# Chunk starts set by ScalarE and low weight parts by identity products, in a linear-attention and mixer kernel

## The chip, the cores and the metric

The kernel runs on one core of a Trainium2 chip. The core has a TensorE (PE, matmuls into PSUM; its weight loads are counted apart as PEld), a VectorE (DVE), a ScalarE (ACT), a GpSimd (POOL) and a SyncE (SP), whose queue issues all DMAs here. Each engine works through its own list of instructions in order and waits on semaphores for the others. The metric is device time in microseconds, the median of three runs.

## The reference

Three layers follow each other, all in fp32, with batch 4, 8 heads, 768 tokens and 48 channels a head:

```python
f = 1.0 / (1.0 + np.exp(-f_logit))
for t in range(S):                                     # gated linear attention
    state = f[:, :, t, :, None] * state + einsum('bhd,bhe->bhde', k[:, :, t], v[:, :, t])
    y[:, :, t] = einsum('bhd,bhde->bhe', q[:, :, t], state)
h = np.maximum(x @ w_in, 0.0)                          # x: [4, 768, 384], w_in: [384, 1024]
u, v = h[..., :512], h[..., 512:]
v_s = einsum('ts,bsd->btd', w_spatial, normalised(v)) + b_spatial[None, :, None]
x = (u * v_s) @ w_out
h = np.maximum(x.T @ w_tok1, 0.0) @ w_tok2             # per batch, over tokens
u = x + h.T
out = u + np.maximum(u @ w_ch1, 0.0) @ w_ch2           # 384 -> 1536 -> 384
```

## The kernel before

**Numbers.** Dense products are made from two parts of each fp32 operand: a high part `h` in the type fp32r (which TensorE takes in one pass) and a low part `l = a - h`. `mm3` (L149) issues three products for one: high by high, high by low, low by high. The weights arrive as fp64 (all but `w_sp`), so `rounded` (L57) makes an fp32 weight from two words with three DVE operations (L65, L68, L78), two on ACT (L72, L74) and one on POOL (L73). `split_weight` (L100) then casts the high part on ACT (L115, for `w_sp` L121) and subtracts on an engine that its caller names (L124): POOL for `w_in` (9 pieces, 6 of 384 columns and 3 of 256), `w_sp` (12 of 384) and `w_out` (4 of 384). `staged` (L129) runs such a piece in four steps, so that a few pieces are under way together; their staging tiles (`wsa`, `wst`) have three buffers each.

**Attention.** A unit is one batch, one half of the tokens (384) and one pair of heads, 4 x 2 x 4 = 32 units. Its input `fkq` holds logits, keys and queries, 128 x 3 x 384, brought by one DMA (the first unit's by three). ACT takes the sigmoid of the logits into `fs` (L369). `chunked` (L218) cuts the 384 tokens into three chunks of 128. DVE copies each chunk's first decay into `first` (L225, 128 x 3), sets those places of `fs` to zero (L226), and scans (L227): the running product `pc` of the decays restarts at each chunk. POOL copies the three end products to `pend` (L230). DVE clamps them at 1e-20 (L232), inverts them (L233) into `last`, scans backwards from them (L234) and multiplies keys and queries by both scans in one operation (L237, 128 x 768). PE transposes the keys (L243), multiplies keys by queries (L252), builds the state increments (L266, L267), and adds the outputs up in `py` (L297, L302, L308); POOL masks the 128 x 128 products (L257); DVE carries the state along (L277, L288, L290). The result is split into `xh` (ACT, L380) and `xl` (DVE, L381). `least`, the smallest of the end products, is looked at once, and a second, general program runs only if it is below 1e-20; it does not run here.

**First phase.** `s1` makes the hidden layer from `xh`, `xl` (products `pv`, `pu`), `s23` mixes tokens with `wsph`, `wspl` (`ps`), gates, and multiplies by `wouth`, `woutl` (`px`). Attention of the next batch, `s1` and `s23` of this batch and the conversion of weights are woven together by step counts (`weave`, L141). Batch 0's first attention half is woven with `w_in`, the second with `w_sp`, the first loop pass with `w_out`; the fp64 weights of the second phase are rounded during the passes that follow.

**Second phase.** Token and channel products of the last layer, from about 470 us on. It is a dense stream of matmuls with three-part products.

**What sets the order.** The program is built by a layer that assigns semaphores and, from a modelled timeline at build time, also chooses in which order each engine's instructions stand. A change of one instruction therefore moves others. The tag `m` of PSUM (pool `ps_m`, three buffers) serves `pv`, `pu`, `ps` and `px`.

Of the kernel before, what the change touches and what calls it, by code (L numbers as in the profile page):

```python
# [18 lines left out]
def tile_kernel(ctx, tc, fkqs, v, w_in, w_sp, b_sp, w_out, w_t1, w_t2, w_c1, w_c2, out):  # L19
# [28 lines left out]
    ident = const.tile([P, P], F32, name="ident")  # L48
    least = const.tile([P, 1], F32, name="least")
    flag = const.tile([1, 1], I32, name="flag")  # L50
# [48 lines left out]

    def split_weight(pool, stage, src, name, n, cols, eng, first=0, order=None):  # L100

        wide = src.dtype == mybir.dt.uint64
        h = pool.tile([P, n, cols], F32R, name=name + "h")
        l = pool.tile([P, n, cols], F32R, name=name + "l")
        if wide:
            src = src.bitcast(U32)
        srcr = src.rearrange("(n p) c -> n p c", p=P)

        def piece(i, c0, width):
            sl = (slice(None), i, slice(c0, c0 + width))  # L110
            at = stage.tile([P, WST], U32, tag="wsa", name=f"{name}sa{i}{c0}")
            a = at[:, :width]
            if wide:
                a = yield from rounded(stage, a, srcr[first + i], c0, width, f"{name}{i}{c0}")
                nc.scalar.copy(h[sl], a)  # L115
                yield
            else:
                a = f32(a)
                nc.sync.dma_start(out=a, in_=srcr[first + i][:, c0 : c0 + width])
                yield  # L120
                nc.scalar.copy(h[sl], a)  # L121
                yield
                yield
            eng.tensor_tensor(out=l[sl], in0=a, in1=f32(h[sl]), op=ALU.subtract)  # L124

        where = [(i, c0, min(WST, cols - c0)) for i in range(n) for c0 in range(0, cols, WST)]
        return h, l, [partial(piece, *x) for x in (order(where) if order else where)]

    def staged(pieces):  # L129

        gens = []

        def step(n):
            if n < len(pieces):
                gens.append(pieces[n]())
            for g in gens[max(0, n - 3) : n + 1]:
                next(g, None)

        return [partial(step, n) for n in range(len(pieces) + 3)]

# [16 lines left out]
    def body(general):  # L157
# [32 lines left out]
        if not general:  # L190
# [3 lines left out]
            )  # L194
            nc.gpsimd.memset(nhalf, -0.5)
        first, last = (attp.tile([P, W], F32, name=x) for x in ("first", "last"))
        states = [attp.tile([P, 128], F32, name=f"state{i}") for i in range(4)]
# [20 lines left out]
        def chunked(u, b, hf, p, fs, fkq, vt):  # L218
            ki, qi = fkq[:, 1, :], fkq[:, 2, :]
            n0 = hf * NCW  # L220
# [3 lines left out]
            gc, pc = pg[:, 0, :], pg[:, 1, :]  # L224
            nc.vector.tensor_copy(first[:, ::C], fs[:, :W:C])  # L225
            nc.vector.memset(fs[:, ::C], 0.0)  # L226
            nc.vector.tensor_tensor_scan(  # L227
                out=pc, data0=fs[:, :W], data1=first, initial=0.0, op0=ALU.mult, op1=ALU.add
            )
            nc.gpsimd.tensor_copy(pend[:, b * NP + p, n0 : n0 + NCW], pc[:, C - 1 :: C])  # L230
            ends = last[:, C - 1 :: C]
            nc.vector.tensor_scalar(out=ends, in0=pc[:, C - 1 :: C], scalar1=LOW, scalar2=None, op0=ALU.max)  # L232
            nc.vector.reciprocal(ends, ends)  # L233
            nc.vector.tensor_tensor_scan(  # L234
                out=gc[:, ::-1], data0=fs[:, W:0:-1], data1=last[:, ::-1], initial=0.0, op0=ALU.mult, op1=ALU.add
            )
            nc.vector.tensor_tensor(out=fkq[:, 1:, :], in0=fkq[:, 1:, :], in1=pg, op=ALU.mult)  # L237
            yield
# [75 lines left out]
        def scanned(u, b, hf, p, fs, fkq, vt):  # L314
# [15 lines left out]
            last = at3.tile([P, D], F32, tag=f"z{p}", name=f"z{u}")  # L330
            ki, qi, fs = fkq[:, 1, :], fkq[:, 2, :], fs[:, :W]
            for e in range(D):
# [19 lines left out]
        def att_unit(b, hf, p):  # L352

            u = f"{b}{hf}{p}"
            t0 = hf * W
            fkq = at3.tile([P, 3, W], F32, tag="fkq", name=f"fkq{u}")
            if (b, hf, p) == (0, 0, 0):
                for i in range(3):
                    nc.sync.dma_start(out=fkq[:, i, :], in_=fkqs[b, p, hf, :, i, :])
            else:  # L360
                nc.sync.dma_start(out=fkq, in_=fkqs[b, p, hf])
# [6 lines left out]
            fs = at2.tile([P, W + 1], F32, tag="fs", name=f"fs{u}")  # L368
            nc.scalar.activation(fs[:, :W], fkq[:, 0, :], AF.Sigmoid)  # L369
            core = scanned if general else chunked  # L370
# [75 lines left out]
        def s23(b):  # L446
# [39 lines left out]


        winh, winl, steps = split_weight(
            wr, wst, w_in, "win", NK, DFF, nc.gpsimd, order=lambda x: sorted(x, key=lambda y: -y[1])
        )  # L490
        weave(att(half(0, 0)), staged(steps))
        bb = const.tile([P, S], F32, tag="bb", name="bb")
        nc.sync.dma_start(out=bb, in_=b_sp.unsqueeze(0).to_broadcast([P, S]))
        wsph, wspl, st_a = split_weight(wl, wst, w_sp, "wsp", NCH, S, nc.gpsimd)
        wouth, woutl, st_b = split_weight(wl, wst, w_out, "wout", NJ, DM, nc.gpsimd)
        s10, a01, sa = s1(0, 0), att(half(0, 1)), staged(st_a)
# [250 lines left out]
```

## Time and profile before

| | |
|---|---|
| median of 3 runs | 825.38 us (825.36 to 826.94) |
| the profiled execution's own time | 828.73 us |
| its span in the trace | 827.0 us |
| PE busy | 765.1 us (93%) |
| DVE busy | 443.2 us (54%) |
| ACT busy | 274.6 us (33%) |
| POOL busy | 240.0 us (29%) |
| chain that ended last | PE 66%, DVE 17%, DMA 6%, issue 5% |

The shares of the whole span say little, since the stages differ: the 40 slices of the page and the busy times by stretch show which engine has no room in which stretch. Durations of matmuls in the trace overlap, since they are pipelined; the distance from one start to the next is what one costs. The chain names, going back from the last instruction, what released each step; "issue" is time in which the profile shows no releaser.

### The profile page before, as it was taken

What the parts mean: (1) busy time and instruction counts of PE and PEld (TensorE: products, weight loads), DVE (VectorE), ACT (ScalarE), POOL (GpSimd) and SP (SyncE); (2) the same over time, 40 slices, a digit from 0 to 9 for tenths busy, and PEclk for the clock granted to TensorE, in tenths of its full rate; (3) what the DMA queues carried; (4) which work ended last, traced back from release to release, by engine and by line L of the source; (5) the groups of instructions that cost most, each with busy time, mean ns of one, the idle gap of its engine ahead of it and who ended that gap; (6) DMA issues with size and microseconds to landing.
All of it is one profiled execution on the core that took longest, in us unless ns stands there. A gap on an engine that the chain in (4) does not pass through costs nothing.

```text
span 827.0 us, 12669 instructions
## 1 busy us (share of the span) xinstructions
PE 765.1 (93%) x4785; PEld 707.5 (86%) x4785; DVE 443.2 (54%) x916; ACT 274.6 (33%) x590; POOL 240.0 (29%) x290
## 2 busy tenths in 40 slices
PE   3468698999989999999999999999999999999996
PEld 2357577787778888899899999999999999999996
DVE  6997979989898874864464352122122212222211
ACT  4554535445452433323552341112112311111110
POOL 5786835535471112110580340004001210001000
PEclk9659689999989999999999999999999999999999
DMA  7473446575644331120341230002000200000000
GB/s 240 132 219 112 146 127 207 169 255 181 220 132 149 107 104 39 58 82 23 117 134 48 87 115 30 1 1 86 1 29 1 86 1 29 1 1 31 3 28 33
DMA packets 39846, 73.67 MB, mean 89 GB/s; under 512 B 5216, under 2 KB 29664, under 8 KB 39776
## 3 DMA queue, kind: packets, MB, share of 16 engines
q1 hardware_dynamic: 39776, 72.77, 27.7%
q8 instruction: 40, 0.66, 0.3%
q14 instruction: 30, 0.25, 0.1%
HBM read 54.66 MB, written 15.73 MB: 85 GB/s over the span
## 4 chain that ended last, share of the span: by engine, by line
PE 66%; DVE 17%; DMA 6%; issue 5%; POOL 2%; ACT 1%; SPq 1%; DVEq 0%; POOLq 0%; ACTq 0%
PE po L644 18%; PE p L155 8%; PE p L153 8%; PE p L154 8%; PE ps L153 2%; PE ps L155 2%; PE ps L154 2%; PE pa L252 2%; DVE pg L227 2%; PE px L153 2%; PE px L154 2%; PE py L302 2%; PE px L155 2%; PE py L308 1%; DVE state L277 1%
## 5 line engine op out<-in xcount | busy, mean ns | idle before, releaser
L632 DVE SCALAR_TENSOR_TENSOR hl<-p,hh 128x384 fp32r<-128x384 f32 x96 | 53.4, 557 | 189.6 <-ACT hh L631 189.6
L631 ACT ACTIVATE hh<-p 128x384 fp32r<-128x384 f32 x96 | 47.1, 492 | 198.1 <-PE p L155 198.1
L644 PE MATMUL po<-hl,wc2h 128*128 128x384 f32 x288 | 97.2, 338 | 0.0
L644 PE MATMUL po<-hh,wc2l 128*128 128x384 f32 x288 | 96.7, 336 | 0.0
L655 POOL TENSOR_TENSOR us<-uh,ul 128x384 f32<-128x384 f32 x24 | 24.4, 1027 | 233.4 <-DVE ul L615 216.1
L644 PE MATMUL po<-hh,wc2h 128*128 128x384 f32 x288 | 75.0, 336 | 0.0
L153 PE MATMUL ps<-wsph,vh 128*128 128x384 f32 x192 | 66.6, 348 | 0.0
L155 PE MATMUL ps<-wsph,vl 128*128 128x384 f32 x192 | 65.9, 345 | 0.0
L154 PE MATMUL ps<-wspl,vh 128*128 128x384 f32 x192 | 65.6, 342 | 0.0
L155 PE MATMUL p<-uh,wc1l 128*128 128x384 f32 x192 | 65.0, 338 | 0.0
L154 PE MATMUL p<-ul,wc1h 128*128 128x384 f32 x192 | 64.7, 337 | 0.0
L153 PE MATMUL p<-uh,wc1h 128*128 128x384 f32 x192 | 64.2, 338 | 0.0
L257 POOL TENSOR_SCALAR_AFFINE_SELECT am<-am 128x384 f32<-128x384 f32 x64 | 42.9, 686 | 58.9 <-ACT am L256 58.7
L644 PEld LDWEIGHTS po<-hl,wc2h 128*128 128x128 f32 x288 | 54.1, 188 | 0.0
L644 PEld LDWEIGHTS po<-hh,wc2l 128*128 128x128 f32 x288 | 54.1, 188 | 0.0
L644 PEld LDWEIGHTS po<-hh,wc2h 128*128 128x128 f32 x288 | 52.3, 188 | 0.0
L302 PE MATMUL py<-fkq,state 112*112 112x128 f32 x160 | 37.4, 332 | 13.4 <-DVE state L277 10.9
L302 PEld LDWEIGHTS py<-fkq,state 112*112 112x112 f32 x160 | 26.6, 201 | 23.0 <-DVE state L277 15.9
L252 PE MATMUL pa<-fkq 48*128 48x128 f32 x384 | 40.7, 328 | 0.0
L615 DVE TENSOR_TENSOR ul<-p,uh 128x384 fp32r<-128x384 f32 x24 | 13.4, 557 | 47.6 <-ACT uh L614 47.6
L252 PEld LDWEIGHTS pa<-fkq 48*128 48x128 f32 x384 | 30.7, 215 | 9.0 <-issue 5.1
L153 PE MATMUL pu<-xh,winh 128*128 128x384 f32 x96 | 34.9, 364 | 3.6 <-ACT r L420 2.8
(407 smaller groups left out, 1944.2 us busy)
## 6 DMA issues: line engine op xcount, KB each, us to landing
fkq<-in_fkq SPq DMA_DIRECT2D x31, 576.0 KB, 4.5
vt<-in_v SPq DMA_DIRECT2D x8, 576.0 KB, 6.2
x1d<-xs SPq DMA_DIRECT2D x24, 192.0 KB, 2.0
xf<-x1d SPq DMA_DIRECT2D x12, 384.0 KB, 4.1
out<-ot SPq DMA_DIRECT2D x24, 192.0 KB, 2.5
wspsa<-in_w_sp SPq DMA_DIRECT2D x12, 192.0 KB, 3.2
wc1d<-wc1da SPq DMA_DIRECT2D x12, 192.0 KB, 2.0
wc2d<-wc2da SPq DMA_DIRECT2D x12, 192.0 KB, 2.1
```

The source lines that it names most:

```text
L153: nc.tensor.matmul(ps, lh, rh, start=first and i == 0, stop=False, **kw)
L154: nc.tensor.matmul(ps, lh, rl, start=False, stop=False, **kw)
L155: nc.tensor.matmul(ps, ll, rh, start=False, stop=i == n - 1, **kw)
L227: nc.vector.tensor_tensor_scan(out=pc, data0=fs[:, :W], data1=first, initial=0.0, op0=ALU.mult, op1=ALU.add)
L252: nc.tensor.matmul(pa[j][:, c, :], ki[64 * j : 64 * j + D, sl], qi[64 * j : 64 * j + D, sl], start=True, stop=True)
L257: nc.gpsimd.affine_select(out=am[j], in_=am[j], compare_op=ALU.is_ge, fill=0.0, base=0, pattern=[[0, NCW], [1, C]], channel_multiplier=-1,)
L302: nc.tensor.matmul(py[:112, c, :], now[c][:112, :112], qi[:112, c * C : (c + 1) * C], start=c == 0, stop=False, skip_group_check=True,)
L615: nc.vector.tensor_tensor(out=ul[:, c, tsl], in0=ps, in1=f32(uh[:, c, tsl]), op=ALU.subtract)
L631: nc.scalar.activation(hh, ps, AF.Relu)
L632: nc.vector.scalar_tensor_tensor(out=hl, in0=ps, scalar=0.0, in1=f32(hh), op0=ALU.max, op1=ALU.subtract)
L644: nc.tensor.matmul(po[c], l[:, ft, csl], r, start=ft == 0 and x == 0, stop=ft == NF - 1 and x == 2)
L655: nc.gpsimd.tensor_tensor(out=us[c], in0=f32(uh[:, c, tsl]), in1=f32(ul[:, c, tsl]), op=ALU.add)
```

## The change

**Chunk starts.** The host lays the input of a unit out as one row of 3 x 384 + 1 + 3 = 1156 numbers in place of 3 x 384: keys, queries, then the logits with -100 at the three chunk starts and one more behind the end, then the three original logits of the chunk starts. ACT's sigmoid covers 385 columns (new L377) and gives a decay of practically zero at the starts by itself; a second, three-column sigmoid on ACT (new L379) writes the true first decays into `first`. The DVE copy (L225), the DVE memset (L226) and the DVE clamp (L232) are gone; the reciprocal (new L240) reads the end products directly.

**Low weight parts.** For `w_in`, `w_sp` and `w_out` the subtraction on POOL is replaced by two matmuls into a `ps_m` buffer, identity by `a` in fp32 (new L130) and minus identity by `h` in fp32r (new L131), and by a copy of the result to `l` on ACT (new L133). `minus` is made once on ACT from `ident` (new L205). A piece now has five steps, and `staged` runs five.

```diff
-            eng.tensor_tensor(out=l[sl], in0=a, in1=f32(h[sl]), op=ALU.subtract)
+            if eng is not nc.tensor:
+                eng.tensor_tensor(out=l[sl], in0=a, in1=f32(h[sl]), op=ALU.subtract)
+                return
+            ps = psum.tile([P, W], F32, tag="m", name=f"{name}pl{i}{c0}")[:, :width]
+            nc.tensor.matmul(ps, ident, a, start=True, stop=False)
+            nc.tensor.matmul(ps, minus, h[sl], start=False, stop=True)
+            yield
+            nc.scalar.copy(l[sl], ps)
...
+            nc.scalar.mul(minus, ident, -1.0)
...
-            nc.vector.tensor_copy(first[:, ::C], fs[:, :W:C])
-            nc.vector.memset(fs[:, ::C], 0.0)
...
-            ends = last[:, C - 1 :: C]
-            nc.vector.tensor_scalar(out=ends, in0=pc[:, C - 1 :: C], scalar1=LOW, scalar2=None, op0=ALU.max)
-            nc.vector.reciprocal(ends, ends)
+            nc.vector.reciprocal(last[:, C - 1 :: C], pc[:, C - 1 :: C])
...
-            nc.scalar.activation(fs[:, :W], fkq[:, 0, :], AF.Sigmoid)
+            nc.scalar.activation(fs, fkq[:, 2 * W : 3 * W + 1], AF.Sigmoid)
+            starts = fs[:, :W:C] if general else first[:, ::C]
+            nc.scalar.activation(starts, fkq[:, 3 * W + 1 :], AF.Sigmoid)
...
-            wr, wst, w_in, "win", NK, DFF, nc.gpsimd, order=lambda x: sorted(x, key=lambda y: -y[1])
+            wr, wst, w_in, "win", NK, DFF, nc.tensor, order=lambda x: sorted(x, key=lambda y: -y[1]), psum=ps_m
...
-        wsph, wspl, st_a = split_weight(wl, wst, w_sp, "wsp", NCH, S, nc.gpsimd)
-        wouth, woutl, st_b = split_weight(wl, wst, w_out, "wout", NJ, DM, nc.gpsimd)
+        wsph, wspl, st_a = split_weight(wl, wst, w_sp, "wsp", NCH, S, nc.tensor, psum=ps_m)
+        wouth, woutl, st_b = split_weight(wl, wst, w_out, "wout", NJ, DM, nc.tensor, psum=ps_m)
```

**How instructions move.** The numbers behind a name are buffers; the lines are each kernel's own. First DVE's list at the fourth unit of attention (`fs_344`, in the changed kernel `fs_365`), where `w_in` is also being rounded (`winsa`). Before:

```order
L225 COPY first<-fs_344 128x3
L277 SCALAR_TENSOR_TENSOR state_127<-z_316,pend,own 112x2x48
L290 SCALAR_TENSOR_TENSOR z_319<-z_316,pend,pk_305 112x48
L226 MEMSET fs_344 128x4
L65 TENSOR_SCALAR winsa_339<-win00st 128x384
L227 SCALAR_TENSOR_TENSOR pg_346<-fs_344,first 128x384
L68 SCALAR_TENSOR_TENSOR winsa_339<-win00st,winsa_339 128x384
L232 TENSOR_SCALAR last<-pg_346 128x3
L65 TENSOR_SCALAR winsa_363<-win10st 128x384
L233 RECIPROCAL last<-last 128x3
L68 SCALAR_TENSOR_TENSOR winsa_363<-win10st,winsa_363 128x384
L234 SCALAR_TENSOR_TENSOR pg_346<-fs_344,last 128x384
```

And the same unit in the changed kernel's DVE list:

```order
L297 SCALAR_TENSOR_TENSOR z_323<-z_320,pend,pk_309 112x48
L236 SCALAR_TENSOR_TENSOR pg_368<-fs_365,first 128x384
L66 TENSOR_SCALAR winsa_336<-win00st 128x384
L240 RECIPROCAL last<-pg_368 128x3
L69 SCALAR_TENSOR_TENSOR winsa_336<-win00st,winsa_336 128x384
L241 SCALAR_TENSOR_TENSOR pg_368<-fs_365,last 128x384
L66 TENSOR_SCALAR winsa_360<-win10st 128x384
```

The three small operations are gone; the scans stand between the same neighbours.

Next PE's list where attention's second half (batch 0) meets `w_sp`, from the end of the fifth unit on. Before:

```order
L308 MATMUL py_461<-am_439,vt_146 64x128
L308 MATMUL py_461<-am_440,vt_146 48x128
L266 MATMUL pk_561<-vt_508,kn_542 64x48
L267 MATMUL pk_561<-vt_508,kn_542 48x48
L266 MATMUL pk_561<-vt_508,kn_542 64x48
L267 MATMUL pk_561<-vt_508,kn_542 48x48
L243 MATMUL pt_606<-ident,fkq_523 128x112 x2
L252 MATMUL pa_611<-fkq_523 128x128
```

And in the changed kernel's PE list, behind the same state increments:

```order
L130 MATMUL wsppl_620<-wspsa_554,ident 128x384
L130 MATMUL wsppl_646<-wspsa_576,ident 128x384
L130 MATMUL wsppl_677<-wspsa_606,ident 128x384
L131 MATMUL wsppl_620<-wsph,minus 128x384
L131 MATMUL wsppl_646<-wsph,minus 128x384
L131 MATMUL wsppl_677<-wsph,minus 128x384
L250 MATMUL pt_626<-ident,fkq_542 128x112 x2
L259 MATMUL pa_631<-fkq_542 128x128
```

Three pieces' products, all three buffers of `ps_m`, now stand between one unit's state increments and the next unit's transposes.

## Rows read from the trace of the kernel before

**Rows 1.** Page, busy tenths in 40 slices of 20.7 us: DVE and granted clock
```profile
DVE  6997979989898874864464352122122212222211
PEclk9659689999989999999999999999999999999999
```

**Rows 2.** Busy time by stretch, all engines; columns as in the first line
```profile
core 0: us, PE busy (x) PEld busy (x) DVE busy (x) ACT busy (x) POOL busy (x), PEclk, DMA share, GB/s
0.00:45.00 45.00, 19.13 (x136) 13.91 (x136) 37.92 (x75) 20.89 (x47) 28.01 (x44) 0.79 0.60 190
45.00:110.00 65.00, 50.71 (x329) 39.36 (x329) 58.26 (x117) 31.37 (x72) 44.73 (x51) 0.70 0.48 145
110.00:240.00 130.00, 116.84 (x761) 97.97 (x760) 118.16 (x258) 66.28 (x147) 63.33 (x76) 0.94 0.61 196
240.00:420.00 180.00, 178.43 (x1256) 157.41 (x1256) 118.24 (x278) 67.67 (x150) 46.61 (x79) 1.00 0.28 86
420.00:827.00 407.00, 399.96 (x2310) 398.82 (x2308) 110.64 (x190) 88.36 (x176) 57.31 (x46) 1.00 0.11 36
```

**Rows 3.** Busy time by stretch of DVE alone
```profile
12.00:45.00 33.00, 32.81 (x62) 0.71 0.53 164
80.00:110.00 30.00, 29.48 (x58) 0.66 0.40 115
```

**Rows 4.** Chain that ended last, 44 to 76 us: start, length, what
```profile
46.78 2.29 issue
...
64.84 4.10 DMA fkq<-in_fkq
```

**Rows 5.** DVE groups, 0 to 240 us: count, busy us, mean ns, idle before
```profile
L232 DVE TENSOR_SCALAR last<-pg 128x3 f32<-128x3 f32 x20 | 8.2, 411 | 0.3
...
L225 DVE COPY first<-fs 128x3 f32<-128x3 f32 x20 | 6.9, 346 | 12.6 <-ACT fs L369 12.4
...
L226 DVE MEMSET fs<- 128x4 f32 x20 | 1.2, 62 | 0.4
```

**Rows 6.** Timeline of the first 10 us: start, length, what, idle before
```profile
0.79 1.28 ACT L369 ACT_TABLE_LOAD   x1 [0.79 <-PEq L738]
...
3.32 0.52 ACT L369 ACTIVATE fs<-fkq 128x384 f32<-128x384 f32 x1 [1.24 <-DMA fkq<-in_fkq]
...
3.95 0.17 DVE L225 COPY first<-fs 128x3 f32<-128x3 f32 x1 [3.95 <-ACT fs L369]
...
4.28 0.96 DVE L227 TENSOR_TENSOR_SCAN pg<-fs,first 128x384 f32<-128x384 f32 x1
...
5.35 0.17 DVE L232 TENSOR_SCALAR last<-pg 128x3 f32<-128x3 f32 x1
...
9.35 0.29 DVE L65 TENSOR_SCALAR winsa<-win0768st 128x256 uint32<-128x256 uint32 x1 [1.64 <-DMA win0768st<-in_w_in]
```

**Rows 7.** POOL groups, 0 to 110 us: the subtractions of line 124
```profile
L124 POOL TENSOR_TENSOR wspl<-wspsa,wsph 128x384 fp32r<-128x384 f32 x12 | 15.1, 1271 | 8.7 <-ACT wsph L121 8.6
...
L124 POOL TENSOR_TENSOR winl<-winsa,winh 128x384 fp32r<-128x384 f32 x6 | 7.1, 1200 | 2.1 <-ACT winh L115 2.1
L124 POOL TENSOR_TENSOR woutl<-woutsa,wouth 128x384 fp32r<-128x384 f32 x4 | 5.3, 1316 | 0.1
...
L124 POOL TENSOR_TENSOR winl<-winsa,winh 128x256 fp32r<-128x256 f32 x3 | 4.2, 1406 | 2.2 <-ACT winh L115 2.2
```

**Rows 8.** Timeline of all engines at 32.2 us: start, length, what
```profile
32.22 1.00 POOL L124 TENSOR_TENSOR winl<-winsa,winh 128x384 fp32r<-128x384 f32 x1 [1.04 <-ACT winh L115]
32.27 1.76 DVE L227 TENSOR_TENSOR_SCAN pg<-fs,first 128x384 f32<-128x384 f32 x1
```

**Rows 9.** Timeline of PE, 56 to 70 us: records of one fp32 product
```profile
59.50 1.19 PE L302 MATMUL py<-fkq,state 112*112 112x128 f32 x4
...
67.08 0.82 PE L302 MATMUL py<-fkq,state 112*112 112x128 f32 x6
```

**Rows 10.** Groups of the whole span by shape: two ACT operations
```profile
L245 ACT COPY kn<-pt 128x224 f32<-128x224 f32 x16 | 5.5, 344 | 7.1 <-PE pt L243 7.1
...
L121 ACT CAST wsph<-wspsa 128x384 fp32r<-128x384 f32 x12 | 6.0, 512 | 2.6 <-DMA wspsa<-in_w_sp 2.6
```

More of the change, by code (lines that the diff above doesn't have):

```diff
@@ L48, in tile_kernel @@
     ident = const.tile([P, P], F32, name="ident")
+    minus = const.tile([P, P], F32R, name="minus")
     least = const.tile([P, 1], F32, name="least")
@@ L98, in tile_kernel, with split_weight @@
     kept = {}
-    def split_weight(pool, stage, src, name, n, cols, eng, first=0, order=None):
+    def split_weight(pool, stage, src, name, n, cols, eng, first=0, order=None, psum=None):
         wide = src.dtype == mybir.dt.uint64
@@ L135, in step @@
                 gens.append(pieces[n]())
-            for g in gens[max(0, n - 3) : n + 1]:
+            for g in gens[max(0, n - 4) : n + 1]:
                 next(g, None)
-        return [partial(step, n) for n in range(len(pieces) + 3)]
+        return [partial(step, n) for n in range(len(pieces) + 4)]
     def weave(main, *fillers):
@@ L218, in chunked @@
         def chunked(u, b, hf, p, fs, fkq, vt):
-            ki, qi = fkq[:, 1, :], fkq[:, 2, :]
+            kq = fkq[:, : 2 * W].rearrange("p (a t) -> p a t", a=2)
+            ki, qi = kq[:, 0, :], kq[:, 1, :]
             n0 = hf * NCW
@@ L236, in chunked @@
             )
-            nc.vector.tensor_tensor(out=fkq[:, 1:, :], in0=fkq[:, 1:, :], in1=pg, op=ALU.mult)
+            nc.vector.tensor_tensor(out=kq, in0=kq, in1=pg, op=ALU.mult)
             yield
@@ L330, in scanned @@
             last = at3.tile([P, D], F32, tag=f"z{p}", name=f"z{u}")
-            ki, qi, fs = fkq[:, 1, :], fkq[:, 2, :], fs[:, :W]
+            ki, qi, fs = fkq[:, :W], fkq[:, W : 2 * W], fs[:, :W]
             for e in range(D):
@@ L355, in att_unit @@
             t0 = hf * W
-            fkq = at3.tile([P, 3, W], F32, tag="fkq", name=f"fkq{u}")
+            fkq = at3.tile([P, 3 * W + 1 + NCW], F32, tag="fkq", name=f"fkq{u}")
             if (b, hf, p) == (0, 0, 0):
-                for i in range(3):
-                    nc.sync.dma_start(out=fkq[:, i, :], in_=fkqs[b, p, hf, :, i, :])
+                for i in (2, 0, 1):
+                    x = slice(i * W, (i + 1) * W + (i == 2) * (1 + NCW))
+                    nc.sync.dma_start(out=fkq[:, x], in_=fkqs[b, p, hf, :, x])
             else:
@@ L723 @@
     rows = np.concatenate([pair[:-1], last], 2).reshape(-1)
+    f = heads(f_logit, 20.0)
+    cut = np.pad(f, [(0, 0)] * 4 + [(0, 1)], constant_values=-100.0)
+    cut[..., ::128] = -100.0
     arrays = {
-        "fkq": np.stack([heads(f_logit, 20.0), heads(k, 0.0), heads(q, 0.0)], 4),
+        "fkq": np.concatenate([heads(k, 0.0), heads(q, 0.0), cut, f[..., ::128]], -1),
         "v": np.ascontiguousarray(np.transpose(v, (0, 2, 1, 3))).reshape(b, s, h * d),
```

## The prediction

> **What bounds the kernel now.** I read the page's 40 slices first: DVE stands at 8 or 9 tenths in most slices of the first third and at 1 or 2 in the second half, and the granted clock of PE is low only in the first quarter, with 5 or 6 tenths in slices two and three [rows 1]. The stretches say where time can be won [rows 2]. From 240 us on PE is busy 178.4 of 180 and then 400.0 of 407 us; there nothing that helps another engine counts. Before 240 us PE stands idle for 25.9 + 14.3 + 13.2 = 53 us. In 12 to 45 us and in 80 to 110 us DVE has no gap at all, 32.8 of 33 and 29.5 of 30 us [rows 3], and from 110 to 240 us it is busy for 91% while PE has 10% free [rows 2]. So the front 240 us go by DVE's list, with one exception: between 45 and 80 us the chain runs through attention's products on PE, with steps of "issue" of 2.29 us, and through an exposed load of 4.10 us [rows 4]. A microsecond taken from DVE before 240 us is worth nearly one; PE work added there is free where DVE binds and is paid where the chain runs through PE.
>
> **The three small DVE operations.** Of the 32 units 20 fall into the first 240 us, and in them the copy, the memset and the clamp took 6.9 + 1.2 + 8.2 = 16.3 us of DVE [rows 5]. Part of that is not their own work: the first unit's copy and clamp took 0.17 us each [rows 6], the means are 346 and 411 ns [rows 5]. Bare, the three cost (0.17 + 0.06 + 0.17) x 20 = 8.0 us. What is above that is time spent waiting for POOL, and could pass to the next DVE operation. So the gain lies between 8 and 16.3 us; I take 12, because the reciprocal that now comes next has the same small shape and is unlikely to inherit the whole wait. The 12 units after 240 us are covered by PE, which has 1.6 us free there [rows 2]: nothing. If PE were not full there, they would give 12 x 0.40 = 4.8 us more.
>
> **The small sigmoid.** It takes the place of the copy in the chain of a unit: load, sigmoid, first decays, scan. ACT's smallest group in the rows is a copy of 224 columns with 344 ns [rows 10], so the three-column one costs between 0 and 0.34 us, against a copy and memset of 0.17 + 0.06 us bare. DVE waited 12.4 us for the sigmoid in those 20 units [rows 5]; the change leaves that wait, and moves it to the scan. Per unit on the chain that is between -0.23 and +0.11 us; I count 0 and keep -5 to +2 us for the 20 units. Since `first` is one buffer, the small sigmoid must also wait until DVE has scanned the unit before; in ACT's new list it stands directly behind the large one, which itself follows that unit's key copy by way of PE, so the scan is long done. The first unit pays once: ACT must make `minus` from the identity and load a second table of 1.28 us before the sigmoid that started at 3.32 us [rows 6]. The sigmoid waited 1.24 us for its load anyhow, and DVE stood idle for 1.64 us at 9.35 us [rows 6]; so 0 to 1 us, and I take 0.3. The Trainium skill's "ScalarE: Activation LUTs" (What ACT_TABLE_LOAD costs) gives a switch of tables some 1.4 us of draining on top of the load; the row shows the load of 1.28 us alone, and by that page this term would be about 1 us larger.
>
> **POOL without the 25 subtractions.** POOL loses 15.1 + 7.1 + 5.3 + 4.2 = 31.7 us out of 28.0 + 44.7 busy before 110 us [rows 2, 7]. POOL itself is not the bound. But its operations lengthen DVE's: a scan that ran beside a subtraction took 1.76 us [rows 8], the first unit's, with POOL not subtracting, 0.96 us [rows 6]: 0.80 us. If none of the 25 delays a DVE operation that binds, the gain is 0; if each costs 0.80, it is 20 us. Some DVE operations do not collide, and those that leave this POOL operation alone will meet the next one (mask, rounding). I take 0.3 us each, 7 us, nearer to the lower end.
>
> **25 products on PE.** The trace has no fp32 product of 384 columns. One of 128 columns is two records: six records took 0.82 us at 67 us, four took 1.19 us at 59.5 us [rows 9], that is 0.27 and 0.60 us a product; the first is at a clock near 2.4 GHz, the second at 1.2 GHz. Three times that is 0.82 or 1.79 us for 384 columns. The lower end is two records at the pace of the dense stretch, 407 / 2310 = 0.176 us [rows 2], so 0.35 us. The product with `minus` adds 0.18 us at full clock and 0.35 at half. So a piece is between 0.5 us and 2.1 us of PE, 13 to 53 us for 25; at 0.9 us, near the full-clock row, some 21 us net of the three narrower pieces. The nine pieces of `w_in` stand in units that run before 45 us, where DVE has no gap and PE has 25.9 us free: hidden, and if DVE ceased to bind there they would cost up to 9 x 2.1 = 19 us. The four of `w_out` fall behind 80 us, under DVE again. The twelve of `w_sp` stand between attention's products, three pieces in a row, in the stretch where the chain runs through PE. They can cost 0 to 12 x 2.1 = 25 us; I take half of them at 0.9, 5 us, because DVE is busy 58.3 of 65 us in that stretch too [rows 2].
>
> **New waits on PE and ACT.** PE's product with `minus` waits for the cast on ACT, and in PE's list the next unit's transposes, keys by queries and outputs are queued behind it; before, POOL waited so, with only the masks queued behind. ACT copies 25 more results, near 0.51 us each as the casts of `w_sp` [rows 10], 12.8 us; ACT is busy 31.4 of 65 us from 45 to 110 us [rows 2]. Behind such a copy waits ACT's own list: the copies of keys and masks' inputs, which PE waits for. Free if they fill ACT's gaps, 6 us if half of them sit in front of something waited for. I take 1 us. The larger load (1156 for 1152 columns) is nothing.
>
> **The sum.** -12 (small DVE operations) - 7 (POOL beside DVE) + 5 (products of `w_sp`) + 1 (waits on ACT) + 0.3 (start) = -12.7 us. Against the profiled execution's own 828.73 us that is 816.0; the median of the runs is 3.35 us lower, and the same step from it gives **812.7 us**, 1.5% faster.
>
> **Rivals.** (a) *PE becomes the bound from 45 to 110 us, and it is slower.* The granted clock was 0.70 in that stretch [rows 2] and half of 2.4 GHz around 50 us [rows 1]; if it stays there, twelve pieces in threes with 2.1 us each put 25 us on the chain, against -12 - 7 + 1.3: +7, 828 to 833 us. For it: the three buffers of `ps_m` are all taken at once, and the chain is on PE there already. Against it: PE has 14.3 us idle there, and fills it. It decides once the twelve cost more than 18 us together, 1.5 us each. (b) *The gain is taken back.* After the small operations DVE no longer binds from 110 to 240 us; there PE, with 13 us free, and the loads bind, and of 19 us only what the start of the program wins remains, less the 5 on PE: within 1.6 us of 825.4. (c) *POOL's lock is gone altogether.* If the subtractions delayed DVE by 0.80 us each [rows 8], the term is -20: -12 - 20 + 6.3 = -25.7, 799.7 us. The Trainium skill's "SBUF — State Buffer" (Who interferes with whom) says that DVE and POOL share a pair of ports as an exclusive lock, so that the loser blocks for a whole instruction; the row of 1.76 against 0.96 us agrees, and by that page the lock would make this case the likelier one, were it not that POOL's other operations take it too. (d) *The copy's time only turns into a wait for the small sigmoid.* Then of the 12 us only the clamp's part remains, about 6 us, and the change gives -6 - 7 + 6.3 = -6.7, 818.7 us. A schedule made anew could also shift a stage by a few microseconds to either side; I put this into the range.
>
> **Chances.** Forecast (803 to 817) 0.48; (c) 0.14; (d) 0.14; (b) 0.10; (a) 0.14. A difference below 0.2% (1.65 us) cannot be told from none here. So faster 0.48 + 0.14 + 0.14 = 0.76, same 0.10, slower 0.14. The range reaches down to 799, over most of (c), and up to 828, over (b) and the lower part of (a): about 0.83.
>
> **What would show it.** In the profile after: DVE busy before 240 us down by about 20 us from 214; no small DVE operation but the reciprocal around the scans; the scans' mean closer to 0.96 us; PE full from some 225 us on. The identity product near 0.8 us of PE at 2.4 GHz, its two records together. The granted clock between 45 and 110 us above 0.70, since PE has more to do. Wrong if DVE has new gaps before 110 us that end with PE's `pt`, `pk` or `py`, if PE waits for the casts of `wsph`, or if the small sigmoid waits for a scan.

## The result and the profile after

The changed kernel takes **818.93 us** in the median of its runs (818.64 to 820.29), beside 825.99 us of the kernel before on the same chip: a ratio of 0.9914, interval 0.9899 to 0.993, that is 7.1 us or 0.86% less. It was forecast at 812.7 us with a range of 799 to 828 and a chance of 0.76 for faster by over 0.2%: the side and the range hold, the step is a little over half of the 12.7 us of the sum. The profiled execution took 819.0 us, its span 817.2 us. The one of the kernel before lay 3.35 us above its median, so of the 9.7 us between the two profiles some 3 belong to that one execution.

The busy tenths in 40 slices of 20.4 us, on the page of the changed kernel, to be laid beside [rows 1]:

```profile
DVE  6968599899898846673552532122122212221211
...
PEclk9899899999999999999999999999999999999998
```

And the stretches, beside [rows 2] (columns as there):

```profile
0.00:45.00 45.00, 31.57 (x205) 21.54 (x206) 36.96 (x71) 29.57 (x70) 19.84 (x38) 0.92 0.69 225
45.00:110.00 65.00, 59.53 (x427) 45.78 (x428) 45.88 (x97) 35.97 (x90) 20.95 (x35) 0.95 0.44 133
110.00:240.00 130.00, 120.39 (x785) 104.13 (x784) 118.99 (x238) 69.63 (x160) 67.96 (x74) 0.95 0.61 197
240.00:420.00 180.00, 176.79 (x1203) 157.06 (x1203) 113.74 (x233) 72.55 (x167) 53.91 (x82) 0.99 0.30 93
```

From 45 to 110 us DVE went from 58.3 to 45.9 of 65 us busy and POOL from 44.7 to 21.0; PE rose from 50.7 to 59.5. From 110 to 240 us little looks different: DVE is busy for 119 of 130 us as it was for 118. Where the time was won, and where some of it went again, is told by when the same piece of work is done. The table gives the end of an instruction in us, read from the records of each kernel's trace (the second column of times is a run of the kernel before with the order of its lists chosen anew, experiment 4; e1 and e2 are the two parts of the change alone, experiment 1; e12 is experiment 3). The last row says by how much the profiled execution lay above or below the median of its kernel's runs; it belongs beside every difference at the end:

| | before | before, other order | e1 starts | e2 weights | e12 | after |
|---|---|---|---|---|---|---|
| fourth unit's keys and queries scaled | 39.5 | 39.5 | 36.9 | 39.3 | 33.1 | 33.2 |
| ReLU of batch 0's third `pv` product (end of its first half) | 85.9 | 85.6 | 80.1 | 75.9 | 78.1 | 69.9 |
| ReLU of batch 0's sixth `pv` product (end of its second half) | 125.2 | 124.7 | 121.4 | 115.9 | 115.3 | 111.8 |
| fourth gated block of batch 0, cast to `gh` | 157.4 | 156.9 | 157.3 | 148.6 | 149.0 | 143.5 |
| sixteenth unit's keys and queries scaled | 184.3 | 183.5 | 172.3 | 163.5 | 161.2 | 159.2 |
| batch 1 written | 313.1 | 311.2 | 311.9 | 305.6 | 296.6 | 302.1 |
| end | 827.0 | 825.5 | 826.7 | 820.9 | 811.7 | 817.2 |
| this execution against its kernel's median | +3.4 | +1.3 | -0.1 | -1.2 | -1.9 | +0.1 |

The changed kernel is 13 us ahead at 112 us and 10 us at the end; against the other order of the kernel before it is 13 and 8 us. By these marks the gain is made in the first 110 us, and 3 to 5 us of it are lost again, most of them before 313 us. It depends on the mark how early: batch 0's last `pu` product, the other half of its hidden layer, is through its ReLU at 132.0 us before and 124.1 us after, only 8 us ahead. That most of the gain is there early, and that none is added behind 145 us, holds by either mark.

The chain that ended last shows what is late there now. Here it is from 78 to 90 us (start, length, what):

```profile
79.85 0.82 DVE woutsa L79
80.68 3.11 DMA wout30st<-in_w_out
83.81 0.04 ACTq L73
83.85 0.04 issue
83.90 0.55 ACT wout30st L73
84.45 0.45 ACT wout10st L75
...
85.58 2.66 DMA wt1d00st<-in_w_t
88.27 0.04 ACTq L73
88.30 0.04 issue
88.35 0.43 ACT wt1d00st L73
88.78 0.40 ACT wouth L116
89.18 0.38 ACT yh L390
89.55 0.39 ACT am L263
89.94 0.04 issue
89.99 2.03 PE pa L259 x11
```

ACT works its list in order, and in it the rounding's copy (new L73) waits twice for a weight to arrive; behind it stand the copies of the masks' inputs (new L263), and PE waits for these. Where DVE bound before, loads and ACT's order now do; of the whole chain DVE fell from 17% to 10% and DMA rose from 6% to 10%.

### The profile page after: what moved, and what is told of

It reads as the page before. It is cut to its first block, busy times and chain, and to the rows that moved or that the text cites. A ratio compares the mean times of both kernels' runs of the same rounds, so it can differ in the third digit from the quotient of the medians.

```text
span 817.2 us, 12758 instructions
## 1 busy us (share of the span) xinstructions
PE 777.3 (95%) x4860; PEld 716.3 (88%) x4860; DVE 420.3 (51%) x820; ACT 289.1 (35%) x649; POOL 211.1 (26%) x265
## 4 chain that ended last, share of the span: by engine, by line
PE 71%; DVE 10%; DMA 10%; issue 4%; ACT 2%; SPq 1%; POOL 1%; DVEq 0%; ACTq 0%; POOLq 0%
PE po L654 19%; PE p L164 8%; PE p L162 8%; PE p L163 8%; DMA fkq<-in_fkq 3%; PE ps L162 3%; PE ps L164 3%; PE ps L163 3%; PE pa L259 2%; PE py L309 2%; PE py L315 2%; PE px L162 2%; PE px L163 1%; PE px L164 1%; DVE pg L236 1%
## 5 line engine op out<-in xcount | busy, mean ns | idle before, releaser
L264 POOL TENSOR_SCALAR_AFFINE_SELECT am<-am 128x384 f32<-128x384 f32 x64 | 46.9, 748 | 69.7 <-ACT am L263 69.5
L236 DVE TENSOR_TENSOR_SCAN pg<-fs,first 128x384 f32<-128x384 f32 x32 | 33.3, 1039 | 22.2 <-ACT first L379 22.1
L259 PEld LDWEIGHTS pa<-fkq 48*128 48x128 f32 x384 | 30.5, 204 | 12.3 <-issue 4.3
L162 PEld LDWEIGHTS ps<-wsph,vh 128*128 128x128 f32 x192 | 37.1, 193 | 2.4 <-issue 1.6
L625 DVE TENSOR_TENSOR ul<-p,uh 128x384 fp32r<-128x384 f32 x24 | 13.4, 557 | 47.6 <-ACT uh L624 47.6
L163 PEld LDWEIGHTS ps<-wspl,vh 128*128 128x128 f32 x192 | 37.0, 193 | 0.5 <-issue 0.2
```

The lines of the kernel that those rows point to most:

```text
L162: nc.tensor.matmul(ps, lh, rh, start=first and i == 0, stop=False, **kw)
L163: nc.tensor.matmul(ps, lh, rl, start=False, stop=False, **kw)
L236: nc.vector.tensor_tensor_scan(out=pc, data0=fs[:, :W], data1=first, initial=0.0, op0=ALU.mult, op1=ALU.add)
L259: nc.tensor.matmul(pa[j][:, c, :], ki[64 * j : 64 * j + D, sl], qi[64 * j : 64 * j + D, sl], start=True, stop=True)
L264: nc.gpsimd.affine_select(out=am[j], in_=am[j], compare_op=ALU.is_ge, fill=0.0, base=0, pattern=[[0, NCW], [1, C]], channel_multiplier=-1,)
```

## The experiments

Each kernel ran beside the kernel before on the same chip. Between experiments the ratios to it are compared. In the expectations of experiment 1, A is the prediction's account (DVE's time won, POOL's relief) and B that the products' gain is a higher granted clock; from experiment 2 on A, B and C are other theories, told in experiment 1, behind its four runs.

### 1. The two parts alone, and what stands in the second

The first kernel has only the new chunk starts; the low parts stay on POOL.

```diff
-            wr, wst, w_in, "win", NK, DFF, nc.tensor, order=..., psum=ps_m
+            wr, wst, w_in, "win", NK, DFF, nc.gpsimd, order=...
```

> Only the chunk starts of the change: new host layout, small sigmoid on ACT, no copy, memset and clamp on DVE; the low weight parts stay on POOL. Theory A (the gain comes from DVE's list, by fewer small operations and by POOL no longer beside it): about half of the 7.1 us, 820 to 823 us, with DVE busy before 240 us lower by 8 to 16 us and the scans' mean in the front still at 1.06 us. Theory B (the gain comes from PE's granted clock, which the identity products raise between 20 and 110 us): 824 to 826 us, granted clock from 45 to 110 us still near 0.70.

Measured: 828.53 us, 1.0033 (1.0019 to 1.0047): **slower**, which neither theory had. The second has only the low parts on PE.

```diff
-            nc.scalar.activation(fs, fkq[:, 2 * W : 3 * W + 1], AF.Sigmoid)
-            starts = fs[:, :W:C] if general else first[:, ::C]
-            nc.scalar.activation(starts, fkq[:, 3 * W + 1 :], AF.Sigmoid)
+            nc.scalar.activation(fs[:, :W], fkq[:, 0, :], AF.Sigmoid)
+            nc.vector.tensor_copy(first[:, ::C], fs[:, :W:C])
+            nc.vector.memset(fs[:, ::C], 0.0)
```

> Only the low weight parts of the change: identity products on PE and a copy on ACT in place of 25 subtractions on POOL; attention as before. Theory A: the other half, 820 to 823 us. Theory B: nearly all of it, 818 to 820 us, with the granted clock from 45 to 110 us at 0.9 or more.

Measured: 823.87 us, 0.9976 (0.9958 to 0.9994). The third takes the second and leaves the products out; POOL is spared all the same, and the low part is a copy of the weight, not its low part.

```diff
-            nc.tensor.matmul(ps, ident, a, start=True, stop=False)
-            nc.tensor.matmul(ps, minus, h[sl], start=False, stop=True)
             yield
-            nc.scalar.copy(l[sl], ps)
+            nc.scalar.copy(l[sl], a)
```

> As the kernel with only the low weight parts changed, but the identity products are left out: ACT copies the weight itself into the low part, so the low part isn't subtracted at all. POOL is rid of its 25 operations, ACT has its 25 copies, PE has nothing more. Theory A: faster than with the products, by the 5 us that I had put down for them, 815 to 819 us. Theory B: slower than with the products, 822 to 826 us, since the granted clock from 45 to 110 us stays near 0.70.

Measured: 823.73 us, 0.9974 (0.9956 to 0.9993). The fourth is the kernel before, POOL subtracting, with the products made beside it and not used.

```diff
-            eng.tensor_tensor(out=l[sl], in0=a, in1=f32(h[sl]), op=ALU.subtract)
+            nc.gpsimd.tensor_tensor(out=l[sl], in0=a, in1=f32(h[sl]), op=ALU.subtract)
+            ps = psum.tile([P, W], F32, tag="m", ...)[:, :width]
+            nc.tensor.matmul(ps, ident, a, start=True, stop=False)
+            nc.tensor.matmul(ps, minus, h[sl], start=False, stop=True)
```

> The kernel before, with the 25 subtractions still on POOL, and the identity products issued on PE as well, their result unused. PE's extra work alone. Theory A: it only costs, 826 to 832 us. Theory B: faster than the kernel before, 819 to 823 us, granted clock from 45 to 110 us at 0.9 or more.

Measured: 833.24 us, 1.009 (1.0065 to 1.0114). Its granted clock from 45 to 110 us was 0.87 against 0.70 [rows 2], and still it is the slowest: whatever the clock gave back, it did not pay for the products, which cost 7.4 us in this kernel.

So the parts alone come to +2.7 and -2.0 us, +0.7 together, where the change as a whole brings -7.1. Three theories were left: that what the starts win is taken back from 110 to 240 us, where the rounding of weights fills DVE (A); that a freshly chosen order moves such times by some us whatever the edit (B); that the parts need each other (C, first in the form that the products' clock lets DVE's gain through). Experiments 2 to 4 are about that.

How the starts alone could bring nothing is seen on DVE's and POOL's groups from 0 to 110 us (count, busy us, mean ns, idle before). In the kernel before:

```profile
L237 DVE TENSOR_TENSOR fkq<-fkq,pg 128x768 f32<-128x768 f32 x11 | 12.7, 1152 | 0.1
L234 DVE TENSOR_TENSOR_SCAN pg<-fs,last 128x384 f32<-128x384 f32 x11 | 12.1, 1103 | 0.2
...
L232 DVE TENSOR_SCALAR last<-pg 128x3 f32<-128x3 f32 x11 | 5.6, 511 | 0.3
...
L257 POOL TENSOR_SCALAR_AFFINE_SELECT am<-am 128x384 f32<-128x384 f32 x20 | 14.0, 710 | 2.4 <-ACT am L256 2.4
```

In the kernel with the starts alone:

```profile
L231 DVE TENSOR_TENSOR_SCAN pg<-fs,last 128x384 f32<-128x384 f32 x11 | 13.9, 1264 | 0.2
L234 DVE TENSOR_TENSOR fkq<-fkq,pg 128x768 f32<-128x768 f32 x11 | 12.9, 1170 | 0.1
...
L230 DVE RECIPROCAL last<-pg 128x3 f32<-128x3 f32 x11 | 1.9, 169 | 0.2
...
L254 POOL TENSOR_SCALAR_AFFINE_SELECT am<-am 128x384 f32<-128x384 f32 x20 | 18.9, 960 | 1.3 <-ACT am L253 1.3
```

And with the weights alone, where the clamp is still there:

```profile
L244 DVE TENSOR_TENSOR_SCAN pg<-fs,last 128x384 f32<-128x384 f32 x11 | 10.6, 964 | 0.2
...
L242 DVE TENSOR_SCALAR last<-pg 128x3 f32<-128x3 f32 x12 | 2.2, 187 | 0.2
```

The clamp's mean of 511 ns was at most 187 ns of its own and the rest waiting for POOL: it fell away as soon as POOL stopped subtracting. When instead the clamp was taken away and POOL went on, the reciprocal did not take the wait over (169 ns); the backward scan behind it went from 1103 to 1264 ns, and POOL's masks from 710 to 960 ns.

The same over all instructions: take of each DVE or POOL record what is above the shortest record of its line and shape, and add up what starts before 110 us. That is the time stretched, in us:

| | DVE, before 110 us | POOL, before 110 us |
|---|---|---|
| before | 28.6 | 19.6 |
| before, other order (e6) | 28.3 | 19.0 |
| starts alone (e1; e10) | 29.2; 29.0 | 25.4; 25.2 |
| POOL spared, old starts (e2; e3) | 12.3; 15.7 | 8.0; 12.2 |
| POOL spared, new starts (e12; after; e5) | 15.1; 13.8; 13.4 | 16.4; 10.9; 11.2 |

The starts alone leave DVE's stretched time as it was and put 6 us more on POOL. The Trainium skill's "SBUF — State Buffer" (Who interferes with whom) has DVE and POOL share a pair of ports as an exclusive lock, on which the loser waits for a whole instruction; the rows agree that the two engines hold each other up, and add that such a wait stays with the pair of engines when the instruction on which it was booked is taken away. That a whole instruction is waited for is not read from them. Yet some won time did reach the list: e1 is ahead by 4 to 6 us at 80 to 125 us in the table above. It is gone at 157 us by the cast to `gh` (DVE's subtraction behind that cast still stands 2 us ahead, 159.1 us against 161.3). DVE had hardly a gap there (19.7 of 20 us busy from 140 to 160 us), and the sixteenth unit, work of the next batch, came 12 us earlier while the gated block of batch 0 came at nearly the same time: what DVE won went into attention of the next batch. That nothing waited for it yet is how I read these marks; no run shows it by itself.

### 2. The rounding of the second-phase weights held back

If DVE's fullness from 110 to 240 us is what takes gains back, then moving other work out of that stretch should keep them. POOL copies one number from the newest unit's end products into the staging tile ahead of each load, so the rounding follows attention's pace. It is added to the changed kernel, to the kernel before, and to the one with the starts alone; the changed kernel also ran unchanged once more.

```diff
         st = stage.tile([P, WST, 2], U32, tag="wst", name=f"{name}st")
+        if after is not None:
+            nc.gpsimd.tensor_copy(f32(st[:, :1, 0]), after)
...
             nc.gpsimd.tensor_copy(pend[:, b * NP + p, n0 : n0 + NCW], pc[:, C - 1 :: C])
+            newest.append(pend[:, b * NP + p, n0 : n0 + 1])
```

> The changed kernel once more, beside the one before on the same chip. If its 818.9 us (0.9914 of the time before) belongs to the kernel and its order, it comes out at 817 to 821 us and 0.989 to 0.994. If it was a lucky chip or hour, nearer to 0.998, the sum of the two parts measured alone (1.0033 and 0.9976).

Measured: 818.7 us, 0.9918 (0.9904 to 0.9932). The result belongs to the kernel.

> The changed kernel, and the rounding of second-phase weights held back: before the load of such a piece POOL copies one number from the end products of the newest attention unit into the staging tile, so that a piece cannot start before that unit; in DVE's list the last piece now stands at the 31st unit instead of the 24th. Theory A (the gain of the starts is taken back from 110 to 240 us, where that rounding fills DVE, ACT and the loads while PE still has some 10 us idle): those 10 us of PE idle shrink to 3 to 6, span shorter by 4 to 8 us than the changed kernel's, 811 to 815 us. Theory B (each new order of the lists moves the time by some us to either side, whatever the edit): 815 to 825 us, with no tie to DVE's busy share from 110 to 240 us. If the rounding, now under the full PE from 240 to 420 us, costs there what it frees before: 818 to 821 us.

Measured: 823.41 us, 0.9962 (0.9941 to 0.9982): 4.7 us slower than without.

> The kernel before with the same holding back and nothing else. Theory A: PE's 13.2 us idle from 110 to 240 us shrink to 5 to 9, 817 to 821 us. Theory B: anything from 820 to 830 us.

Measured: 825.43 us, 0.9996 (0.9985 to 1.0008): no change.

> Only the new chunk starts (as in the experiment that measured 1.0033 alone), with the rounding held back. Theory A: with room on DVE behind 110 us the 4 to 6 us that the starts win before 110 us stay won: 3 to 6 us below the kernel before with the rounding held back. Theory B: the difference to that kernel has no sign of its own, within 4 us to either side; slower than it would fall in with B alone.

Measured: 830.2 us, 1.0062 (1.0049 to 1.0076): 4.8 us slower than e9, the kernel before with the same holding back, and 2.4 us slower than without.

My theory A falls. The stretches of the changed kernel with the rounding held back show how:

```profile
110.00:240.00 130.00, 127.29 (x861) 109.29 (x859) 105.23 (x222) 60.69 (x142) 52.22 (x78) 0.99 0.42 134
240.00:420.00 180.00, 167.06 (x1105) 147.20 (x1102) 122.78 (x251) 77.27 (x179) 69.33 (x104) 0.96 0.40 131
```

PE did get its time back from 110 to 240 us, 127.3 us busy after 120.4, and the second hidden layer of batch 1 was done at 217.2 us against 227.2. But the stretch behind lost more, 167.1 us after 176.8. From 240 to 400 us SP's queue, which issues all loads in order, waited 17.6 us in four waits for the copied number and 15.4 us in five for rounded pieces to store, and loads of weights and of `fkq` lay on the chain there; what each of these cost was not taken apart. The waits alone don't tell it, since in the changed kernel the same queue waited 53.8 us in the same stretch for PE to free the buffers of `fkq`, and was faster. The idle time of PE was moved, not removed. And the starts alone are slower in this order too (e10 against e9), so their loss is not made by the rounding in that one stretch.

### 3. The starts with POOL spared and no products

The third kernel of experiment 1 with the new starts as well, that is, the changed kernel without the identity products:

```diff
-            ps = psum.tile([P, W], F32, tag="m", ...)[:, :width]
-            nc.tensor.matmul(ps, ident, a, start=True, stop=False)
-            nc.tensor.matmul(ps, minus, h[sl], start=False, stop=True)
             yield
-            nc.scalar.copy(l[sl], ps)
+            nc.scalar.copy(l[sl], a)
```

> The changed kernel without the identity products: ACT copies the weight itself into the low part, so POOL is spared and PE gets nothing more (the low part isn't made: the subtraction is left out). With the old chunk starts this measured 823.73 us, the same as with products. Theory C (the products keep PE's granted clock up, 0.95 against 0.65 to 0.85 from 45 to 110 us, and only then what DVE wins is passed on): 823 to 826 us. If the products bring nothing but their cost and starts and a free POOL are enough: 815 to 820 us, with the clock low all the same.

Measured: 815.42 us, 0.988 (0.9855 to 0.9904). With this the six cases stand side by side, in us from the kernel before, as (ratio - 1) x 825.5:

| low parts | old starts | new starts | what the starts do |
|---|---|---|---|
| POOL subtracts | 0 | +2.7 | +2.7 |
| ACT copies, no subtraction | -2.1 | -9.9 | -7.8 |
| PE products and ACT's copy (the change) | -2.0 | -6.9 | -4.9 |

(The change ran twice, the mean of its ratios is 0.9916.) The starts cost time as long as POOL subtracts, and win 5 to 8 us once it doesn't, whether or not PE makes the products. Sparing POOL wins 2 us with the old starts and 12.6 with the new ones. The products cost nothing with the old starts and 3 us with the new ones, where the intervals just touch. The granted clock is not what joins the parts, as this stretch of the fastest of the six shows, with 0.79 against the 0.95 of the changed kernel:

```profile
45.00:110.00 65.00, 53.57 (x357) 42.50 (x358) 49.72 (x104) 39.64 (x100) 30.11 (x36) 0.79 0.51 161
```

Theory C falls with it in the form that the clock makes the gain; that the parts need each other stands.

### 4. The order alone, and the clamp alone

To know what a newly chosen order does, `staged` gets one idle step more, first in the kernel before, then in the changed one. No instruction of the work is added or removed, but the lists come out in another order.

```diff
-            for g in gens[max(0, n - 3) : n + 1]:
+            for g in gens[max(0, n - 4) : n + 1]:
                 next(g, None)
-        return [partial(step, n) for n in range(len(pieces) + 3)]
+        return [partial(step, n) for n in range(len(pieces) + 4)]
```

> The kernel before with one idle step more at the end of each run of weight pieces: no instruction is added, removed or changed, but the pieces are woven in at other places and the order is chosen anew (3484 of some 21,000 lines of PE's two lists differ). It measures what a new order alone does. Theory B (a new order moves the time by some us, whatever the edit, and explains why the parts measured alone sum to +0.7 us and together give -7.1): 2 to 5 us away from the kernel before, to either side. Theory C (order is worth little; the parts need each other): within 1.5 us of it.

Measured: 826.06 us, 1.0001 (0.9986 to 1.0015).

> The same idle step more in the changed kernel, 818.7 to 818.9 us so far. Theory B: 2 to 5 us away from it, and more likely above, at 821 to 824 us, if its order was a lucky one. Theory C: 817 to 820.5 us.

Measured: 819.92 us, 0.9924 (0.9899 to 0.9948). Two other orders moved the time by 0.1 and, by the ratios, 0.7 us. Two are few, and a changed instruction may shift an order more than a step does; but nothing here speaks for an order worth 7 us, and theory B has lost its ground.

Last the clamp, put back into the changed kernel:

```diff
-            nc.vector.reciprocal(last[:, C - 1 :: C], pc[:, C - 1 :: C])
+            ends = last[:, C - 1 :: C]
+            nc.vector.tensor_scalar(out=ends, in0=pc[:, C - 1 :: C], scalar1=LOW, scalar2=None, op0=ALU.max)
+            nc.vector.reciprocal(ends, ends)
```

> The changed kernel with the clamp of the end decays back on DVE (128x3, 20 of them before 240 us, 8.2 us in all in the kernel before). By the prediction's term (a DVE microsecond before 240 us is worth nearly one, bare 0.17 us, at most 0.41 us each): 3.4 to 8.2 us slower, 822 to 827 us. If DVE no longer binds once the rest is gone (it is busy 46 of 65 us from 45 to 110 us in the changed kernel): 0 to 2 us, 818.5 to 821 us.

Measured: 822.23 us, 0.9966 (0.995 to 0.9983), against 0.9918 of the changed kernel: 4 us. Its DVE groups from 0 to 240 us:

```profile
L241 DVE TENSOR_SCALAR last<-pg 128x3 f32<-128x3 f32 x21 | 4.7, 222 | 0.3
L242 DVE RECIPROCAL last<-last 128x3 f32<-128x3 f32 x20 | 3.4, 168 | 0.2
```

Busy 4.7 us, worth 4 us: with POOL spared, the clamp costs what it takes. This kernel also splits the starts. It differs from the one with the low parts alone (0.9976, experiment 1) only by the copy and the memset, which the small sigmoid replaces, and it is 0.8 us faster, with intervals that overlap widely. So of the 4.9 us that the starts win beside the products some 4 are the clamp's, and the copy and the memset, 4.6 us bare, brought nothing that can be told from none.

## Why the prediction was right, and where its sizes were off

**What bounds, and where.** Right: DVE's list set the pace up to 110 us, and the 240 us in front are where the change worked. That DVE "goes by its list" to 240 us was too simple. DVE is as full from 110 to 240 us as before, yet from 112 us on the lead no longer grows; it falls by 3 to 5 us.

**The small DVE operations, -12 us: the step that failed.** The prediction bounded them between the bare 8.0 us and the recorded 16.3, and noted that the surplus is waiting for POOL and "could pass to the next DVE operation". It then took half of that surplus as won, because the reciprocal would not inherit it. The reciprocal indeed did not (154 to 180 ns in all 21 units); the backward scan did, and POOL's masks. The term has no value of its own: +2.7 us with POOL subtracting, -7.8 us with POOL spared and no products, near the bare 8, and -4.9 us with them. The lower bound should have reached below nothing, since the removed operations' neighbours contend in their place. The -4.9 is short of 8 because, beside the products, the clamp brought 4 us and the copy and the memset some 0.8 (experiment 4); the -7.8 was not taken apart. DVE's busy time before 240 us fell by 12.5 us, from 214.3 to 201.8, not by the 20 expected, with one unit more inside it.

**POOL without the subtractions, -7 us.** As a stretch of DVE, undersized: 28.6 us of stretched time before 110 us became 13.8, some 15 us or 0.6 a subtraction, where 0.3 was taken. As time of the kernel it was -2.1 us with the old starts and -12.6 with the new ones, both with ACT's copies in. So the two large terms were added up as if independent, and neither is: each is worth little without the other. Their sum, -19 us, was -9.9 in the kernel without products, ACT's copies in: 9 us too much. The products and waits, +6 in the sum and +3 measured, give 3 of that back, so that -6.9 stood where -12.7 was forecast. That the forecast had the right side is in part luck: the change holds both edits, and of the starts alone the same terms would have said 12 us faster where 2.7 us slower was measured.

**The products, +5 us.** The price of a piece was right. Each identity product in fp32 is two records. The chain between 34 and 49 us has one such product at half clock (granted clock 0.50 from 34.5 to 41 us), and three, with their three partners, at full clock (1.00 from 45 to 49 us):

```profile
34.79 1.58 PE winpl L130 x2
...
46.34 2.13 PE wsppl L130 x6
48.47 0.54 PE wsppl L131 x3
```

2.13 / 3 + 0.18 = 0.89 us a piece at full clock, predicted 0.9; the half-clock records give 1.58 us for the identity product of one piece alone, below the 2.1 for a whole piece. On the path they cost 0 us (old starts, POOL spared) and 3 us (new starts, POOL spared), less than the 5 taken, but 7.4 us where POOL went on subtracting. This term, too, has no value of its own.

**ACT's waits, +1 us.** Not told apart from the relief. The wait that I named, PE behind the cast of `wsph`, did not come: ahead of the new L131 PE stood idle for 0.5 us in all. Another came that I had not named: the masks' inputs behind ACT's wait for loads (85 to 90 us, above).

**The small sigmoid and the start.** As predicted. The first records of ACT and DVE, beside [rows 6]:

```profile
0.79 1.28 ACT L205 ACT_TABLE_LOAD   x1 [0.79 <-PEq L752]
2.10 0.31 ACT L205 ACTIVATE minus<-ident 128x128 fp32r<-128x128 f32 x1
2.42 1.28 ACT L377 ACT_TABLE_LOAD   x1
3.71 0.53 ACT L377 ACTIVATE fs<-fkq 128x385 f32<-128x385 f32 x1
4.14 0.19 ACT L379 ACTIVATE first<-fkq 128x3 f32<-128x3 f32 x1
4.44 0.96 DVE L236 TENSOR_TENSOR_SCAN pg<-fs,first 128x384 f32<-128x384 f32 x1 [4.44 <-ACT first L379]
```

The first scan starts at 4.44 us in place of 4.28, 0.16 us later; 0.3 was taken. The second table costs its 1.28 us and no more. The 1.4 us of draining that the Trainium skill's "ScalarE: Activation LUTs" (What ACT_TABLE_LOAD costs) adds is not in these records: the sigmoid starts 0.01 us after the load's end. The small sigmoid takes 0.19 us, never waits for a scan, and DVE waits for it in four units:

```profile
L379 ACT ACTIVATE first<-fkq x21: 189/192/216, 4.1 to 235.2; 128x3 f32<-128x3 f32 x21
...
  DVE pg L236: 8.9, 4
```

**The rivals.** (a), PE as the bound from 45 to 110 us, did not come in the change; its sign, gaps of DVE that end with PE's work, did appear (4.7 us before 110 us behind `pk` and `py`), but the price stayed at 0.9 us a piece, below the 1.5 from which this rival decides. The kernel with both the subtractions and the products (833.2 us) has the time that this rival named, by another cause: it pays for the products without the relief. (b) came in part: 3 to 5 of 13 us were taken back. (c) was nearest on the lock itself, 0.6 of its 0.80 us a subtraction, and wrong on what that is worth. (d) gave nearly the measured time, 818.7 us, and its split is the nearest of all: 6 us for the clamp, nothing for the copy, where beside the products 4 and some 0.8 us were measured; POOL's relief and the products with their waits -0.7 us together, where the low parts alone brought -2.0. What it lacks is that neither part has such a value by itself, +2.7 us for the starts while POOL subtracts. Its cause, that the copy's time turns into a wait for the small sigmoid, is neither shown nor refuted. DVE's idle time ahead of the first scan before 240 us is 8.9 us in the changed kernel, where 12.4 stood ahead of the copy [rows 5]; but in its other order (e11, first line) and in the fastest kernel (e12, second line) it is larger:

```profile
L236 DVE TENSOR_TENSOR_SCAN pg<-fs,first 128x384 f32<-128x384 f32 x21 | 20.5, 974 | 16.1 <-ACT first L379 16.1
```

```profile
L231 DVE TENSOR_TENSOR_SCAN pg<-fs,first 128x384 f32<-128x384 f32 x22 | 20.9, 949 | 18.4 <-ACT first L374 18.3
```

**What stays open.** Why sparing POOL alone keeps only 2 us, although that kernel is 9 us ahead at 116 to 149 us; and why the starts alone end up behind the kernel before and not level with it. The rows show where the lead goes (the next batch's attention runs ahead; loads and ACT's order take over on the chain), not why just so much. In the profiled executions the starts alone end level with the kernel before (826.7 and 827.0 us), since that one execution of the kernel before lay 3 us above its median; the loss of 2.7 us stands in the runs' medians and ratios. Why the copy and the memset brought nothing beside the products is open as well. A kernel that spares POOL and subtracts at no cost to PE wasn't found; the one of 815.4 us leaves the subtraction out.

## What to carry to other kernels

A wait for a shared resource is booked on whichever instruction meets it: price a removed operation at its shortest record of the same shape, not at its mean, and expect the rest to pass to the next operation unless the other side of the contention goes too. Two edits on the two sides of one contention have no separate prices; run them as a table of two by two before adding them up, and check with an order that is only shuffled how much a new order alone moves. Work handed to an engine with idle time cost less than its busy time here, though not a fixed price: some 21 us of products on PE, by the price of a piece above, cost 0, 3 and 7.4 us in three pairs of kernels. And a lead won in front of a pipeline with fixed orders and load buffers is passed on only in part.

## What the runs showed of the hardware

In all seven profiles with the products, slices 2 to 7 of the granted clock (about 20 to 145 us) stand at 8 or 9 tenths, and each of the seven without them has at least one of these slices at 5 or 6 tenths. Two of the latter, the kernel before in another order and the kernel of experiment 3:

```profile
PEclk9999698999999999999999999999999999999999
```

```profile
PEclk9569699999999999999999999999999999999999
```

How early and how deep the clock falls is not the products' doing alone. The first of these two makes no product, and still its granted clock was 1.00 up to 45 us and 0.87 from 45 to 110 us, against 0.79 and 0.70 of the kernel before [rows 2]:

```profile
0.00:45.00 45.00, 20.41 (x136) 14.94 (x136) 37.85 (x75) 21.05 (x47) 27.40 (x44) 1.00 0.60 191
45.00:110.00 65.00, 51.08 (x332) 39.42 (x332) 58.04 (x117) 31.65 (x72) 45.43 (x51) 0.87 0.46 147
```

So a clock above 0.70, which the prediction gave as a sign, was no sign of the products. Nor did the lower clock cost time here: up to 157 us the two executions reach every mark of the table within 0.5 us of each other. The runs of the kernel before say the same. Over 75 of them, on three chips, the mean granted clock of the whole span lay between 0.952 and 0.963 in 25 and between 0.974 and 0.986 in 50, and the mean time was 825.8 and 825.7 us. The fastest kernel of all, that of experiment 3, had 0.79 from 45 to 110 us.

PE's identity product of 384 columns in fp32 comes as two records and takes 0.71 us in a row of three at full clock, about four times the 0.18 us of the product with `minus` in fp32r.
